# Attention before a mixture of experts: keys loaded two units at a time, their zeros kept in place, and the order of the steps of a unit changed

## The chip, the core and the metric

The kernel runs on one core of a Trainium2 chip. The core has five engines that run on their own and meet at semaphores: TensorE (PE in the profile; its weight loads are PEld), VectorE (DVE), ScalarE (ACT), GpSimd (POOL) and SyncE (SP, which here only issues transfers). Each engine takes its instructions strictly in the order in which they are written. The metric is the time of one execution on the device in microseconds (us); lower is better.

## The reference

Attention over 4 batches of 12 heads, with capped scores, and after it a layer of 8 experts, of which each token uses one:

```python
# q, k, v: (4, 12, 448, 64); cap = 30
scores = q @ k.transpose(0, 1, 3, 2) / sqrt(64)
scores = cap * tanh(scores / cap)
attn = exp(scores - scores.max(-1)) / sum
x = (attn @ v).transpose(0, 2, 1, 3).reshape(1792, 768)

e_idx = argmax(x @ w_gate, 1)          # one expert of 8 per token
h = relu(x[mask] @ w1[e])              # 768 -> 1024
out[mask] = gate_w * eom * (h @ w2[e]) # 1024 -> 768
```

## The kernel before

**Attention** goes over 24 units u; a unit is two heads of one batch (p and p + 6), which lie on the lower and upper 64 partitions. The scores are held with keys on the partitions and queries along a row: 448 keys are three chunks of 128 and a rest of 64. The rests of the two heads are put together into one chunk of 128 whose keys for the other head are zeros, and that is why the key planes have 512 columns and two blocks of zeros. A unit takes these steps:

- `load_k`, `load_q`, `load_v` issue transfers, nearly all from SP. Keys and queries are fetched in pieces of 32 columns (128 bytes), so that DVE can turn them with 32x32 transposes. Queries come for two units in four issues, keys for one unit in six: the rest of the second head is two issues of its own, since it goes to another place in the row than in the tensor. The zeros of the key tiles `kks` are written once, by DVE.
- `t_k(u)` and `t_q(u)` on DVE: one transpose into PSUM (`turned`), one cast to the plane `hi`, one subtraction for `lo` (`planes_of`). The table `TURN` says how many of these run ahead of the unit, before and after the value products. There are five sets of planes.
- `qk(u, s)` on PE: three products (hi·hi, lo·hi, hi·lo) into a PSUM tile, then tanh on ACT (line 369). After the rest, s = 3, one exp over the whole unit follows (line 371).
- `pv(u - 1, c)` on PE: the value products of the unit before (line 379), into the tile u, which ACT or DVE copies out (`u_evac`).
- `presum` on POOL adds the chunks of a unit for the row sums, which PE finishes in `sums`.

`scores` and `half` give out three PSUM tiles in a ring: each taker waits until the last reader of the tile three places before is done. The score tiles, the value products and the steps of the router all take from this ring, in the order in which they are written.

**The router** of a batch (`end_of_batch`) is spread over the units of the next batch: `slots` holds functions that run in places named f, g, h, q and e of a unit. A row step `rws[p]` transposes a unit's output on PE (`row_tr`), scales it on DVE (`row_out`, line 579, tile xr) and puts its store to the tensor xs on a list, which `store_rows` issues from SP at the end of the unit. `gts` transposes the router's products, `logits` and `choose` find each token's expert on DVE, and `rank_mm` and `place` its place in a table, which POOL scatters.

**The seam.** During the last units `early` plans the first five blocks of expert work, `fetch_dma` (fd) reads their rows of the table, `load_raw` (lds) starts the weights from SP, and `gather` on POOL fetches the tokens out of xs. From there on PE multiplies weights that ACT and DVE split into planes (lines 1039, 1040 and 1061).

The main loop and the functions around the change:

Of the kernel before, what the change touches and what calls it, by code (L numbers as in the profile page):

```python
# [22 lines left out]
def tile_kernel(ctx: ExitStack, tc, q, k, v, cap, w_gate, w_ogate, w1, w2, out):  # L23
# [35 lines left out]
    TURN = {6: (1, 2), 8: (1, 2), 10: (2, 2), 13: (1, 2), 14: (1, 2), 15: (1, 2), 16: (1, 2)}  # L59
    KD = DM // 128  # L60
    KF = DFF // 128

# [15 lines left out]
    plp = att.enter_context(tc.tile_pool(name="plp", bufs=5))  # L78
# [20 lines left out]
    BK = 4 * NK  # L99
    NB = S // 32  # L100
# [19 lines left out]
    def load_tails(dst, src, eng):  # L120
        for j in range(2):
            eng.dma_start(out=dst[64 * j:64 * j + 64, NK, j], in_=src[j, SK:S])

    def load_first():
        k_, q_ = heads(k, 0), heads(q, 0)
        load_natural(k0, k_, NK, 128, (nc.sync, nc.scalar))
        load_tails(k0, k_, nc.scalar)
        load_natural(q0, q_, NCH, CP, (nc.sync, nc.scalar))

    def pieces(dst, src, c, eng):  # L130
        x = c % 2
        eng.dma_start(out=dst[32 * c:32 * c + 32],
                      in_=src[:, 32 * x:32 * x + 32].rearrange("(r b) a -> b r a", b=32))

    def load_k(u):
        if u >= NU:
            return
        t, src = kks[u % 4], heads(k, u)
        for c in range(2):
            pieces(t[:, 0:NB], src[0], c, nc.sync)  # L140
        for c in range(2, 4):
            pieces(t[:, 0:BK], src[1, 0:SK], c, nc.sync)
        for c in range(2, 4):
            pieces(t[:, BK + 2:BK + 4], src[1, SK:S], c, nc.sync)

    def load_q(u):
        if u >= NU:
            return
        t = raw1[3 + u // 2 % 3][:, 0:2 * S].rearrange("p (h r a) -> p h r a", h=2, a=32)
        lo = 1 - u % 2  # L150
        for c in range(4):
            h = c // 2 * NP + u % NP
            pieces(t[:, 1 - lo:].rearrange("p h r a -> p (h r) a"), q[u // NP, h:h + lo + 1].rearrange("h s d -> (h s) d"), c, nc.sync)
        for i in range(1 - lo, 2):
            ldq[u + i - (1 - lo)] = t[:, i]

    def load_v(u, eng):
# [9 lines left out]
    zero(k0, nc.vector)  # L167
    load_first()
    for t in kks:
        zero_k(t, nc.vector)  # L170
# [28 lines left out]
    for t in vvs:  # L199
        zero(t, nc.gpsimd)  # L200
# [88 lines left out]
    def part_tile(nm, shape):  # L289
        return plp.tile(shape, F32R, tag=nm, name=nm)  # L290
# [9 lines left out]
    def planes_of(u, ps, nm, n):  # L300
        hi, lo = part_tile(nm + "H", [128, n]), part_tile(nm + "L", [128, n])
        copy(u == 0, hi, ps)
        minus(lo, ps, hi)
        return [hi, lo]

    def t_k(u):
        pl[u] = planes_of(u, turned(kks[u % 4], SK + 128), "K", SK + 128)

    def t_q(u):
        pl[u] += planes_of(u, turned(ldq.pop(u), S), "Q", S)  # L310

    loads = [f for u in range(2, NU) for f in ((load_k, u), (load_q, u)) if f[0] is load_k or u % 2 == 0]
# [27 lines left out]
    def prep_first():  # L340
        pk = tbank([128, SK + 128], "tk0")
        for c in range(NK + 1):
            nc.tensor.transpose(pk[:, c * 128:(c + 1) * 128], k0[:, c].rearrange("p j d -> p (j d)"), ident)
# [3 lines left out]
        pl[0] = planes_of(0, pk, "K", SK + 128) + planes_of(0, pq, "Q", S)  # L347
        scales()


    def qk(u, s):
        KH, KL, QH, QL = pl[u]
        if s == 0:
            pt[u] = ptp.tile([128, 2 * NK + 1, S], F32, tag="pt", name="pt")
        n = 2 if s < NK else 1
        sl = slice(s * 128, (s + 1) * 128)
        if s < NK:
            ps = scores("s")
            for i, (x, y) in enumerate(((KH, QH), (KL, QH), (KH, QL))):
                for j in range(2):  # L360
                    h = slice(64 * j, 64 * j + 64)
                    nc.tensor.matmul(ps[:, j, 0:S], lhsT=x[h, sl], rhs=y[h], start=(i == 0), stop=(i == 2))  # L362
            ps = ps[:, :, 0:S]
        else:
            ps = half("s3")[:, 0:S]
            for i, (x, y) in enumerate(((KH, QH), (KL, QH), (KH, QL))):
                nc.tensor.matmul(ps, lhsT=x[:, sl], rhs=y, start=(i == 0), stop=(i == 2))
            ps = ps.unsqueeze(1)
        nc.scalar.activation(out=pt[u][:, 2 * s:2 * s + n], in_=ps, func=ACTF.Tanh, scale=icap)  # L369
        if s == NK:  # L370
# [69 lines left out]
    def end_of_batch(b):  # L440
# [164 lines left out]
        elif b == B - 2:  # L605
# [732 lines left out]
```

## Time and profile before

| | us |
|---|---|
| three timed runs | 552.52, 554.72, 557.71; median 554.72 |
| the profiled execution | 550.1 |
| its span, first to last instruction | 548.1 |
| PE busy in the span | 502.3 (92%) |
| DVE, ACT, POOL busy | 371.8, 370.3, 284.8 |

The profiled execution is one run; its span is the time between its first and last instruction, and 2.0 us lie around it. In the 40 slices of the profile's page PE is at 9 tenths or more from the middle of the span to shortly before its end, and between 6 and 9 tenths before that; so the page already tells the attention and the experts apart.

### The profile page before, as it was taken

To read this page: it belongs to the slowest core of one execution; us is meant where nothing else is said; L and a number is where in the kernel's file an instruction comes from. 1 tells how busy PE (TensorE), PEld (TensorE's weight loads), DVE (VectorE), ACT (ScalarE), POOL (GpSimd) and SP (SyncE) were. 2 spreads that over 40 slices of the span, in tenths; PEclk is the share of its full clock that TensorE was granted. 3 is DMA by queue.
4 is the path that set the end of the run, shared out by engine and by line. 5 is a ranking of instruction groups with operands and counts; after the bars stand their busy time and mean duration, and the time that the engine had idled before them with its cause. 6 is when DMAs were issued, how large, how long until landed. Compare 5 with 4: busy or idle time off the path is not lost. (4 is left out here: it accounts for less than half of the span.)

```text
span 548.1 us, 10151 instructions
## 1 busy us (share of the span) xinstructions
PE 502.3 (92%) x3077; PEld 346.7 (63%) x3077; DVE 371.8 (68%) x629; ACT 370.3 (68%) x425; POOL 284.8 (52%) x342
## 2 busy tenths in 40 slices
PE   7899799797787979879999999999999999999994
PEld 6354355344333545347899997997879977666692
DVE  5666588685785468348999888786758594546460
ACT  6899578587475667553657987886858686556551
POOL 8999677769665840235715686222637125252001
PEclk9999799899888989979999999999999999999998
DMA  6645565666662224497707932617958959893001
GB/s 137 116 92 101 102 111 109 112 116 94 117 110 61 52 39 80 124 407 200 225 2 287 397 132 88 238 59 256 358 183 308 405 217 387 330 347 133 0 30 47
DMA packets 157772, 91.93 MB, mean 168 GB/s; under 512 B 140418, under 2 KB 140554, under 8 KB 157712
## 3 DMA queue, kind: packets, MB, share of 16 engines
q1 hardware_dynamic: 145792, 57.79, 40.2%
q0 software_dynamic: 8832, 32.74, 16.3%
q10 hardware_dynamic: 3088, 0.71, 0.6%
q8 instruction: 26, 0.43, 0.3%
q14 instruction: 34, 0.28, 0.1%
HBM read 123.68 MB, written 12.04 MB: 248 GB/s over the span
## 5 line engine op out<-in xcount | busy, mean ns | idle before, releaser
L1040 DVE TENSOR_TENSOR wr<-raw,wr 128x768 fp32r<-128x768 f32 (+1 forms) x167 | 171.9, 1066 | 70.0 <-ACT wr L1039 62.4
L1039 ACT ACTIVATE wr<-raw 128x768 fp32r<-128x768 f32 (+1 forms) x167 | 150.4, 935 | 35.9 <-DMA raw<-in_moe_w_dram 12.1
L369 ACT ACTIVATE pt<-s,icap 128x896 f32<-128x896 f32 x96 | 82.2, 912 | 37.3 <-PE s L362 19.9
L379 PE MATMUL u<-pt,vv 128*64 128x448 f32 x384 | 85.5, 591 | 12.3 <-DVE xr L579 6.8
L1061 PE MATMUL py<-wr,hh 128*128 128x384 f32 x352 | 77.3, 340 | 0.0
L1061 PE MATMUL php<-wr,xh 128*128 128x512 f32 x264 | 75.6, 408 | 0.0
L371 ACT ACTIVATE pt<-pt,capc 128x3136 f32<-128x3136 f32 x24 | 69.9, 2911 | 0.8
L1130 POOL DMA_INDIRECT out_dram<-yo,ti x13 | 19.3, 1488 | 95.7 <-ACT yo L1128 72.8
L379 PEld LDWEIGHTS u<-pt,vv 128*64 128x64 f32 x384 | 28.2, 148 | 60.0 <-issue 45.5
L1061 PEld LDWEIGHTS py<-wr,hh 128*128 128x128 f32 x352 | 61.2, 188 | 4.0 <-issue 3.7
L390 POOL TENSOR_TENSOR pa<-pt 128x896 f32<-128x896 f32 x20 | 42.0, 2100 | 27.5 <-ACT pt L371 25.8
L1061 PEld LDWEIGHTS php<-wr,xh 128*128 128x128 f32 x264 | 47.9, 190 | 13.0 <-issue 3.6
L297 DVE STREAM_TRANSPOSE tk<-raw 128x512 f32<-128x512 f32 (+1 forms) x46 | 31.7, 689 | 24.3 <-DMA raw<-in_k_dram 15.5
L391 POOL TENSOR_TENSOR pb<-pa,pt 128x896 f32<-128x896 f32 x20 | 42.0, 2101 | 10.2 <-PE sm L421 8.8
L395 POOL TENSOR_TENSOR pb<-pb,pt 64x448 f32<-64x448 f32 x40 | 45.5, 1137 | 3.1
L1061 PE MATMUL py<-wr,hl 128*128 128x384 f32 x176 | 44.8, 335 | 0.0
L1061 PE MATMUL php<-wr,xl 128*128 128x512 f32 x132 | 41.9, 398 | 0.0
L362 PE MATMUL s<-QH,KH 64*128 64x448 f32 x144 | 30.1, 408 | 7.7 <-DVE ut L402 4.0
L1177 POOL DMA_DIRECT2D rh<-in_moe_w_dram x42 | 23.2, 554 | 22.9 <-DVE wr L1040 13.6
L1061 PEld LDWEIGHTS py<-wr,hl 128*128 128x128 f32 x176 | 31.8, 188 | 0.0
L362 PEld LDWEIGHTS s<-QH,KH 64*128 64x128 f32 x144 | 14.2, 188 | 23.7 <-issue 9.2
L1061 PEld LDWEIGHTS php<-wr,xl 128*128 128x128 f32 x132 | 25.0, 190 | 6.1
(252 smaller groups left out, 788.5 us busy)
## 6 DMA issues: line engine op xcount, KB each, us to landing
raw<-in_moe_w_dram SPq DMA_DIRECT2D x78, 512.0 KB
raw<-in_moe_w_dram SPq DMA_DIRECT2D x104, 384.0 KB
rh<-in_moe_w_dram POOLq DMA_DIRECT2D x18, 512.0 KB
rh<-in_moe_w_dram POOLq DMA_DIRECT2D x24, 384.0 KB
raw<-in_q_dram SPq DMA_DIRECT2D x45, 112.0 KB
vv<-in_v_dram SPq DMA_DIRECT2D x44, 96.0 KB
xs<-xr SPq DMA_DIRECT2D x36, 112.0 KB
raw<-in_k_dram SPq DMA_DIRECT2D x46, 56.0 KB
```

The source lines that it names most:

```text
L297: nc.vector.transpose(out=ps, in_=src.rearrange("p r a -> p (r a)"))
L362: nc.tensor.matmul(ps[:, j, 0:S], lhsT=x[h, sl], rhs=y[h], start=(i == 0), stop=(i == 2))
L369: nc.scalar.activation(out=pt[u][:, 2 * s:2 * s + n], in_=ps, func=ACTF.Tanh, scale=icap)
L371: nc.scalar.activation(out=pt[u], in_=pt[u], func=ACTF.Exp, scale=capc)
L379: nc.tensor.matmul(ups[u][64 * j:64 * j + 64], lhsT=V[:, c, j, :], rhs=P[:, 2 * c + (j if c < NK else 0)], start=(c == 0), stop=(c == NK))
L390: eng.tensor_tensor(out=a, in0=P[:, 0:2], in1=P[:, 2:4], op=ALU.add)
L391: eng.tensor_tensor(out=s1[u], in0=a, in1=P[:, 4:6], op=ALU.add)
L395: eng.tensor_tensor(out=s1[u][h, j], in0=s1[u][h, j], in1=P[h, 2 * NK], op=ALU.add)
L1039: nc.scalar.activation(out=t[:, 0, 0:F], in_=raw, func=ACTF.Copy)
L1040: nc.vector.tensor_tensor(out=t[:, 1, 0:F], in0=raw, in1=t[:, 0, 0:F].bitcast(F32), op=ALU.subtract)
L1061: nc.tensor.matmul(ps[g][:, 0:n], lhsT=st[:, c], rhs=w[:, z, g * n:(g + 1) * n], start=(c == 0 and st is hi and z == 0), stop=(c == (KD, K ...
L1177: nc.gpsimd.dma_start(out=d, in_=rows_of(src, e, w, c), **kw)
```

## The change

1. **Keys.** `load_pair` loads keys as queries were loaded: two units in four issues, into raw1[0] to raw1[2] (they were in raw2[4] to raw2[7]). It may run five units ahead of the turns (keys three, queries four before).
2. **Zeros.** The key planes become ten fixed tiles whose two zero blocks POOL writes once. `k_planes` turns 448 columns instead of 512, and copies and subtracts them in three parts each: 384 columns on all partitions, and twice 64 columns on half of them.
3. **Values.** Two tiles of two units each instead of three of one; the tails of two units come in two issues, so that two units take six issues instead of eight.
4. **Order of a unit.** The rest's products `qk(u, 3)` and their tanh follow directly on the other three; the exp (`expo`) stays behind slots f and g. `TURN` gives its third turn to unit 5 instead of unit 13.
5. **Seam.** `gts`, `logits` and `choose` of the third batch move from places q and e to h of unit 19, ahead of the value products; the row step of p = 5 moves from unit 22 (f) to unit 21 (q), with its store; one step of `early` runs a place sooner.

The diff, cut to its core:

```diff
--- before.py
+++ after.py
-    TURN = {6: (1, 2), 8: (1, 2), 10: (2, 2), 13: (1, 2), 14: (1, 2), 15: (1, 2), 16: (1, 2)}
+    TURN = {5: (1, 2), 6: (1, 2), 8: (1, 2), 10: (2, 2), 14: (1, 2), 15: (1, 2), 16: (1, 2)}
...
-    kks = [raw2[4 + i][:, 0:SK + 128].rearrange("p (r a) -> p r a", a=32) for i in range(4)]
-    vvs = [ldp.tile([128, NK + 1, 2, D], F32, name=f"vv{i}", bufs=1) for i in range(3)]
-    ldq = {}
+    vvs = [ldp.tile([128, 2, NK + 1, 2, D], F32, name=f"vv{i}", bufs=1) for i in range(2)]
+    ldk, ldq = {}, {}
...
-    def pieces(dst, src, c, eng):
-        x = c % 2
-        eng.dma_start(out=dst[32 * c:32 * c + 32],
-                      in_=src[:, 32 * x:32 * x + 32].rearrange("(r b) a -> b r a", b=32))
+    def load_pair(src, u, base, to):
+        t = raw1[base + u // 2 % 3][:, 0:2 * S].rearrange("p (h r a) -> p h r a", h=2, a=32)
+        lo = u % 2
+        for c in range(4):
+            x = c % 2
+            h = c // 2 * NP + u % NP
+            nc.sync.dma_start(
+                out=t[32 * c:32 * c + 32, lo:].rearrange("p h r a -> p (h r) a"),
+                in_=src[u // NP, h:h + 2 - lo, :, 32 * x:32 * x + 32].rearrange("h (r b) a -> b (h r) a", b=32))
+        for i in range(lo, 2):
+            to[u + i - lo] = t[:, i]
 
     def load_k(u):
-        if u >= NU:
-            return
-        t, src = kks[u % 4], heads(k, u)
-        for c in range(2):
-            pieces(t[:, 0:NB], src[0], c, nc.sync)
-        for c in range(2, 4):
-            pieces(t[:, 0:BK], src[1, 0:SK], c, nc.sync)
-        for c in range(2, 4):
-            pieces(t[:, BK + 2:BK + 4], src[1, SK:S], c, nc.sync)
+        load_pair(k, u, 0, ldk)
...
+    def v_tails(u, eng):
+        for j in range(2):
+            h = j * NP + u % NP
+            eng.dma_start(out=vvs[u // 2 % 2][64 * j:64 * j + 64, :, NK, j],
+                          in_=v[u // NP, h:h + 2, SK:S].rearrange("h p d -> p h d"))
+
+    def load_v(u):
         if u < NU:
...
+            v_main(u, nc.sync)
+            v_tails(u, nc.sync)
+            v_main(u + 1, nc.sync)
...
-    for t in kks:
-        zero_k(t, nc.vector)
...
+    kpl = [[plp.tile([128, SK + 128], F32R, name=f"K{i}{z}", bufs=1) for z in "HL"] for i in range(PB)]
+    for hl in kpl:
+        for t in hl:
+            nc.gpsimd.memset(t.bitcast(F32)[0:64, SK + 64:], 0.0)
+            nc.gpsimd.memset(t.bitcast(F32)[64:128, SK:SK + 64], 0.0)
...
+    def k_planes(u, ps):
+        hi, lo = kpl[u % PB]
+        parts = [(hi[:, 0:SK], lo[:, 0:SK], ps[:, 0:SK])]
+        for j in range(2):
+            h, c = slice(64 * j, 64 * j + 64), slice(SK + 64 * j, SK + 64 * j + 64)
+            parts.append((hi[h, c], lo[h, c], ps[h, SK:S]))
+        for x, _, y in parts:
+            copy(u == 0, x, y)
+        for x, z, y in parts:
+            minus(z, y, x)
+        return [hi, lo]
...
-            if u > (tdone[t_k] + 3 if f is load_k else tdone[t_q] + 4):
+            if u > tdone[t_k if f is load_k else t_q] + 5:
...
-        if s == NK:
-            nc.scalar.activation(out=pt[u], in_=pt[u], func=ACTF.Exp, scale=capc)
+
+    def expo(u):
+        nc.scalar.activation(out=pt[u], in_=pt[u], func=ACTF.Exp, scale=capc)
...
-            at = {(-1, "q"): [g0], (0, "f"): [P(sums, EARLY), g1, sums_out], (0, "h"): [t[1]], (0, "q"): gts,
-                  (0, "e"): [logits, choose],
+            at = {(-1, "q"): [g0], (0, "f"): [P(sums, EARLY), g1, sums_out], (0, "h"): [t[1], *gts, logits, choose],
                   (1, "g"): [rank_mm, place, rws[0]], (1, "h"): [place2, enter, scatter], (1, "q"): [rws[1]],
-                  (1, "e"): [nx] * 2,
-                  (2, "g"): [rws[2], rws[3]], (2, "h"): [nx] * 2, (2, "q"): [rws[4]], (2, "e"): [*[nx] * 2, P(set_known, NE)],
-                  (3, "f"): [fd[0], fd[1], *lds[:2], rws[5], store_rows],
+                  (1, "e"): [nx] * 3,
+                  (2, "g"): [rws[2], rws[3]], (2, "h"): [nx], (2, "q"): [rws[4], rws[5]], (2, "e"): [*[nx] * 2, P(set_known, NE)],
+                  (3, "f"): [fd[0], fd[1], *lds[:2]],
...
     for u in range(NU):
-        if u > 2:
-            load_v(u + 1, nc.sync)
+        if u > 2 and u % 2:
+            load_v(u + 1)
         for s in range(NK):
             qk(u, s)
         load_ahead()
+        qk(u, NK)
         before, after = TURN.get(u, (1, 1))
         turn_next(before)
         if 0 < u <= NU - 4:
             presum(u - 1, 1)
         slot(u, "f")
         slot(u, "g")
-        qk(u, NK)
+        expo(u)
```

On PE, at unit 11 (two row steps in place g, trow), before; s is a score tile, s_1289 the rest's, u the value products, sm the row sums:

```order
L362 MATMUL s<-QH,KH 128x448 x2
L362 MATMUL s<-QH,KL 128x448 x2
L362 MATMUL s<-QL,KH 128x448 x2
L574 MATMUL trow<-ident,ut 112x128 x8
L367 MATMUL s_1289<-QH,KH 128x448
L367 MATMUL s_1289<-QH,KL 128x448
L367 MATMUL s_1289<-QL,KH 128x448
L379 MATMUL u<-pt,vv_121 64x448 x8
L421 MATMUL sm<-pb,ohc 32x448 x4
```

The same place of the changed kernel:

```order
L364 MATMUL s<-QH,K1H 128x448 x2
L364 MATMUL s<-QH,K1L 128x448 x2
L364 MATMUL s<-QL,K1H 128x448 x2
L369 MATMUL s_1257<-QH,K1H 128x448
L369 MATMUL s_1257<-QH,K1L 128x448
L369 MATMUL s_1257<-QL,K1H 128x448
L577 MATMUL trow<-ident,ut 112x128 x8
L382 MATMUL u<-pt,vv_121 64x448 x8
L424 MATMUL sm<-pb,ohc 32x448 x4
```

The two row steps now stand between the rest's products and the value products, no longer ahead of the rest.

On DVE, one turn of keys (tk is the transposed tile) and what follows it in unit 10, before:

```order
L297 STREAM_TRANSPOSE tk<-raw_4_116 128x512
L287 CAST KH<-tk 128x512
L293 TENSOR_TENSOR KL<-tk,KH 128x512
L297 STREAM_TRANSPOSE tk<-raw_3_109 128x448
L287 CAST QH<-tk 128x448
L293 TENSOR_TENSOR QL<-tk,QH 128x448
```

And a turn of keys in the changed kernel, in the same unit:

```order
L286 STREAM_TRANSPOSE tk<-raw_0_106 128x448
L276 CAST K3H<-tk 128x384
L276 CAST K3H<-tk 64x64 x2
L282 TENSOR_TENSOR K3L<-tk,K3H 128x384
L282 TENSOR_TENSOR K3L<-tk,K3H 64x64 x2
L500 TENSOR_TENSOR gm<-pg,rec 112x192 x4
```

Three instructions have become seven.

On SP, from unit 21 on to the first weights, before (tc is a block's rows of the table, raw a chunk of weights); the reads of meta between them are left out:

```order
L586 DMA xs<-xr 112x4x64 x6
L118 DMA vv_122<-in_v_dram 128x3x64 x2
L122 DMA vv_122<-in_v_dram 64x64 x2
...
L836 DMA tc<-tab_105 128x2
...
L813 DMA raw_0_106<-in_moe_w_dram 128x1024
...
L813 DMA raw_1_107<-in_moe_w_dram 128x1024
L586 DMA xs<-xr 112x4x64 x2
```

And in the changed kernel:

```order
L108 DMA vv_121<-in_v_dram 128x3x64 x2
L589 DMA xs<-xr 112x4x64 x8
...
L838 DMA tc<-tab_105 128x2
...
L815 DMA raw_0_106<-in_moe_w_dram 128x1024
...
L815 DMA raw_1_107<-in_moe_w_dram 128x1024
```

The last two stores of xs now stand before the table's rows and the first weights, and no value load stands between.


## Rows read from the trace of the kernel before

**Rows 1.** The stretches view: busy us of each engine, granted clock, DMA share.

```profile
core 0: us, PE busy (x) PEld busy (x) DVE busy (x) ACT busy (x) POOL busy (x), PEclk, DMA share, GB/s
...
82.00:126.00 44.00, 39.54 (x246) 19.45 (x242) 34.87 (x70) 32.98 (x31) 31.75 (x23) 0.96 0.60 109
126.00:156.00 30.00, 23.37 (x135) 11.83 (x135) 19.79 (x34) 19.62 (x18) 20.43 (x13) 0.94 0.65 107
156.00:200.00 44.00, 34.94 (x194) 17.51 (x192) 26.36 (x68) 26.48 (x28) 29.47 (x21) 0.88 0.33 64
...
262.00:500.00 238.00, 238.00 (x1525) 197.97 (x1525) 181.50 (x250) 173.32 (x231) 109.87 (x150) 1.00 0.67 247
```

**Rows 2.** The timeline of ACT: start us, us, then [idle before <-releaser].

```profile
28.06 3.31 ACT L369 ACTIVATE pt<-s,icap 128x896 f32<-128x896 f32 x4
...
45.25 2.91 ACT L371 ACTIVATE pt<-pt,capc 128x3136 f32<-128x3136 f32 x1
...
52.24 2.91 ACT L371 ACTIVATE pt<-pt,capc 128x3136 f32<-128x3136 f32 x1
...
63.98 2.91 ACT L371 ACTIVATE pt<-pt,capc 128x3136 f32<-128x3136 f32 x1
...
222.27 2.91 ACT L371 ACTIVATE pt<-pt,capc 128x3136 f32<-128x3136 f32 x1
```

**Rows 3.** The timeline of PE at the value products of five units.

```profile
81.14 3.23 PE L379 MATMUL u<-pt,vv 128*64 128x448 f32 x16
...
99.98 4.67 PE L379 MATMUL u<-pt,vv 128*64 128x448 f32 x16 [2.29 <-DVE xr L579]
...
140.91 4.68 PE L379 MATMUL u<-pt,vv 128*64 128x448 f32 x16 [4.53 <-DVE xr L579]
...
161.06 4.84 PE L379 MATMUL u<-pt,vv 128*64 128x448 f32 x16 [2.15 <-issue]
...
173.74 4.92 PE L379 MATMUL u<-pt,vv 128*64 128x448 f32 x16 [2.31 <-issue]
```

**Rows 4.** The timeline of DVE, three of its steps on keys and queries.

```profile
81.83 0.62 DVE L287 CAST QH<-tk 128x448 fp32r<-128x448 f32 x1
...
138.02 0.73 DVE L297 STREAM_TRANSPOSE tk<-raw 128x512 f32<-128x512 f32 x1 [2.65 <-DMA raw<-in_k_dram]
...
171.47 0.69 DVE L287 CAST KH<-tk 128x512 fp32r<-128x512 f32 x1 [6.19 <-PE s L367]
```

**Rows 5.** The waits of the whole run: total us, times, longest us.

```profile
DVE tk L297 <- DMA raw<-in_k_dram: 15.5, 9, 3.1
...
ACT pt L369 <- PE s L367: 10.3, 11, 1.6
```

**Rows 6.** The timeline of POOL: the last zeroing of value tails, and sums.

```profile
2.21 0.14 POOL L113 MEMSET vv<- 64x64 f32 x1
2.39 0.15 POOL L114 MEMSET vv<- 64x64 f32 x1
...
25.40 2.36 POOL L395 TENSOR_TENSOR pb<-pb,pt 64x448 f32<-64x448 f32 x2
```

**Rows 7.** The source view of line 132, SP's issues: ns min/median/max.

```profile
L132 SPq DMA_DIRECT2D raw<-in_k_dram x138: 311/469/1711, 1.9 to 160.1; - x138
```

**Rows 8.** The timeline of all engines at the seam to the experts.

```profile
194.86 0.22 PE L527 MATMUL trk<-ohb,tri 112*112 112x32 bf16 x1 [3.20 <-DVE ohb L517]
...
223.48 0.91 SPq L586 DMA_DIRECT2D xs<-xr  x2
...
229.80 2.00 POOL L851 DMA_INDIRECT xg<-xs,ti  x1 [8.89 <-DMA tc<-tab]
...
234.20 1.06 ACT L1039 ACTIVATE wr<-raw 128x1024 fp32r<-128x1024 f32 x1 [5.13 <-DMA raw<-in_moe_w_dram]
...
236.99 1.54 PE L863 MATMUL pt_x<-ident,xg 128*128 128x128 f32 x6 [5.39 <-DMA xg<-xs,ti]
...
238.14 0.87 ACT L864 ACTIVATE xh<-pt_x 128x512 fp32r<-128x512 f32 x2 [2.45 <-PE pt_x L863]
```

More of the change, by code (lines that the diff above doesn't have):

```diff
@@ L58, in tile_kernel @@
     UACT = 8
-    TURN = {6: (1, 2), 8: (1, 2), 10: (2, 2), 13: (1, 2), 14: (1, 2), 15: (1, 2), 16: (1, 2)}
+    TURN = {5: (1, 2), 6: (1, 2), 8: (1, 2), 10: (2, 2), 14: (1, 2), 15: (1, 2), 16: (1, 2)}
     KD = DM // 128
     KF = DFF // 128
+    PB = 5
     ctx.enter_context(tc.manual_schedule())
@@ L77, in tile_kernel @@
     att = ExitStack()
-    plp = att.enter_context(tc.tile_pool(name="plp", bufs=5))
+    plp = att.enter_context(tc.tile_pool(name="plp", bufs=PB))
     ldp = att.enter_context(tc.tile_pool(name="ldp", bufs=2))
@@ L118, in load_natural @@
             engs[j].dma_start(out=dst[:, 0:n, j], in_=src[j, 0:n * m].rearrange("(c p) d -> p c d", c=n))
-    def load_tails(dst, src, eng):
-        for j in range(2):
-            eng.dma_start(out=dst[64 * j:64 * j + 64, NK, j], in_=src[j, SK:S])
     def load_first():
@@ L126, in load_first @@
         load_natural(k0, k_, NK, 128, (nc.sync, nc.scalar))
-        load_tails(k0, k_, nc.scalar)
+        nc.scalar.dma_start(out=k0[0:64, NK], in_=k_[:, SK:S].rearrange("j p d -> p j d"))
         load_natural(q0, q_, NCH, CP, (nc.sync, nc.scalar))
-    def pieces(dst, src, c, eng):
-        x = c % 2
-        eng.dma_start(out=dst[32 * c:32 * c + 32],
-                      in_=src[:, 32 * x:32 * x + 32].rearrange("(r b) a -> b r a", b=32))
-    def load_k(u):
-        if u >= NU:
-            return
-        t, src = kks[u % 4], heads(k, u)
-        for c in range(2):
-            pieces(t[:, 0:NB], src[0], c, nc.sync)
-        for c in range(2, 4):
-            pieces(t[:, 0:BK], src[1, 0:SK], c, nc.sync)
-        for c in range(2, 4):
-            pieces(t[:, BK + 2:BK + 4], src[1, SK:S], c, nc.sync)
@@ L146, in load_q @@
-    def load_q(u):
[L147 to L157, printed above, removed]
+    def load_pair(src, u, base, to):
[9 more added lines that the diff above has]
+            to[u + i - lo] = t[:, i]
@@ L158, in load_v, with v_main @@
+    def load_k(u):
+        load_pair(k, u, 0, ldk)
+    def load_q(u):
+        load_pair(q, u, 3, ldq)
+    def v_main(u, eng):
+        load_natural(vvs[u // 2 % 2][:, u % 2], heads(v, u), NK, 128, (eng, eng))
+    def v_tails(u, eng):
[4 more added lines that the diff above has]
+    def load_v(u):
         if u < NU:
-            v_ = heads(v, u)
@@ L199, in tile_kernel @@
     for t in vvs:
-        zero(t, nc.gpsimd)
+        nc.gpsimd.memset(t[0:64, :, NK, 1], 0.0)
+        nc.gpsimd.memset(t[64:128, :, NK, 0], 0.0)
+    kpl = [[plp.tile([128, SK + 128], F32R, name=f"K{i}{z}", bufs=1) for z in "HL"] for i in range(PB)]
[3 more added lines that the diff above has]
+            nc.gpsimd.memset(t.bitcast(F32)[64:128, SK:SK + 64], 0.0)
     load_k(1)
@@ L298, in turned, with q_planes @@
         return ps
-    def planes_of(u, ps, nm, n):
-        hi, lo = part_tile(nm + "H", [128, n]), part_tile(nm + "L", [128, n])
+    def q_planes(u, ps):
+        hi, lo = part_tile("QH", [128, S]), part_tile("QL", [128, S])
         copy(u == 0, hi, ps)
@@ L304, in planes_of @@
         return [hi, lo]
+    def k_planes(u, ps):
[9 more added lines that the diff above has]
+        return [hi, lo]
     def t_k(u):
-        pl[u] = planes_of(u, turned(kks[u % 4], SK + 128), "K", SK + 128)
+        pl[u] = k_planes(u, turned(ldk.pop(u), S))
     def t_q(u):
-        pl[u] += planes_of(u, turned(ldq.pop(u), S), "Q", S)
-    loads = [f for u in range(2, NU) for f in ((load_k, u), (load_q, u)) if f[0] is load_k or u % 2 == 0]
+        pl[u] += q_planes(u, turned(ldq.pop(u), S))
+    loads = [f for u in range(2, NU, 2) for f in ((load_k, u), (load_q, u))]
     tdone = {t_k: 0, t_q: 0}
@@ L340, in prep_first @@
     def prep_first():
-        pk = tbank([128, SK + 128], "tk0")
+        pk = tbank([128, S], "tk0")
         for c in range(NK + 1):
-            nc.tensor.transpose(pk[:, c * 128:(c + 1) * 128], k0[:, c].rearrange("p j d -> p (j d)"), ident)
+            n = min(128, S - c * 128)
+            nc.tensor.transpose(pk[:, c * 128:c * 128 + n], k0[0:n, c].rearrange("p j d -> p (j d)"), ident[0:n, 0:n])
         pq = scores("tq0")[:, 0, 0:S]
@@ L346, in prep_first @@
             nc.tensor.transpose(pq[:, c * CP:(c + 1) * CP], q0[:, c].rearrange("p j d -> p (j d)"), ident[0:CP, 0:CP])
-        pl[0] = planes_of(0, pk, "K", SK + 128) + planes_of(0, pq, "Q", S)
+        pl[0] = k_planes(0, pk) + q_planes(0, pq)
         scales()
@@ L366, in qk @@
             for i, (x, y) in enumerate(((KH, QH), (KL, QH), (KH, QL))):
-                nc.tensor.matmul(ps, lhsT=x[:, sl], rhs=y, start=(i == 0), stop=(i == 2))
+                nc.tensor.matmul(ps, lhsT=x[:, SK:], rhs=y, start=(i == 0), stop=(i == 2))
             ps = ps.unsqueeze(1)
         nc.scalar.activation(out=pt[u][:, 2 * s:2 * s + n], in_=ps, func=ACTF.Tanh, scale=icap)
-        if s == NK:
-            nc.scalar.activation(out=pt[u], in_=pt[u], func=ACTF.Exp, scale=capc)
+    def expo(u):
+        nc.scalar.activation(out=pt[u], in_=pt[u], func=ACTF.Exp, scale=capc)
     def pv(u, c):
         P = pt[u]
-        V = vvs[u % 3]
+        V = vvs[u // 2 % 2][:, u % 2]
         if c == 0:
@@ L967, in tile_kernel @@
         slot(u, "g")
-        qk(u, NK)
+        expo(u)
         if u < 2:
-            load_v(u, nc.scalar)
-        if 0 < u < 3:
-            load_v(u + 1, nc.sync)
+            v_main(u, nc.scalar)
+        if u == 0:
+            v_tails(u, nc.scalar)
+        if u == 1:
+            load_v(2)
         if u > NU - 4:
```

11 lines of the change are left out of this document (removed).

## The prediction, made before the changed kernel ran

> **What bounds the kernel now.** I read the stretches of the span first, then ACT's timeline for the pace of the units, then PE's for its gaps, and last what DVE, POOL and SP were doing at each gap. From 262 to 500 us PE is busy in all 238 us at full clock [rows 1], so the experts cost what they cost, and whatever the attention saves moves the whole of it forward. Up to 228 us no engine is full: between 82 and 200 us PE is busy 39.5 of 44, 23.4 of 30 and 34.9 of 44 us, DVE 34.9, 19.8 and 26.4, ACT and POOL no more than 33 [rows 1]. Units wait there for each other's steps. The last exp starts at 222.27 us [rows 2].
>
> PE's gaps have a pattern. [...] Before, the ring goes s0, s1, s2, row, row, rest, u, so u gets the tile of the first row step and waits until DVE has scaled it; DVE in turn stood behind a turn of keys, which had waited 2.65 us for its transfer (138.02), or for the rest's products to free a key plane (6.19 us, at 171.47) [rows 4].
>
> **The change part by part.**
>
> *Rest ahead of the slots.* Now the ring goes s0, s1, s2, rest, row, row, u: u gets the rest's tile, free as soon as its tanh is done, and xr is wanted only by the next unit's first score tile, one set of value products (3.23 us) later. The plane that DVE waited 6.19 us for is also freed earlier, since the row step no longer stands ahead of the rest. The four gaps cost 2.29 + 1.44, 4.53 + 1.45, 2.15 + 1.61 and 2.31 + 1.69, together 17.5 us (the second number of each is the length above 3.23). PE's whole idle time in the three stretches is 4.5 + 6.6 + 9.1 = 20.2 us, so these are most of it. I take two thirds, 11.7, because the next unit's s0 still waits for xr where DVE is late; the ends are 8 and 17.5. ACT's own wait for the rest, 10.3 us in 11 waits [rows 5], I count at nothing beside it: PE was transposing rows in that time and has to do so in any order. If ACT and not PE were the limit, it would be a gain of up to 10.3.
>
> *Keys in pairs.* Per two units SP issues 4 instead of 12 transfers of keys and 6 instead of 8 of values. At 0.469 us each [rows 7] that is 4.7 us of SP's time per two units. The descriptors stay pieces of 128 bytes and the bytes stay the same, so the transfers themselves get no shorter; what ends DVE's waits for keys (15.5 us in 9 waits [rows 5]) is that a pair may be fetched five units ahead instead of three. DVE's waits are paid in the gaps above and not again: 0. [...]
>
> *Three-part planes.* A cast of 448 columns takes 0.62 us and one of 512 takes 0.69 [rows 4]: 0.0011 us a column and 0.13 fixed. By that 384 columns are 0.55 and 64 are 0.20 (estimates; no row has such a piece of a plane). A turn of keys goes from 0.73 + 2 × 0.69 = 2.11 to 0.66 + 2 × (0.55 + 0.40) = 2.56 us, the 0.66 being 0.73 less 64 columns. Over 23 units DVE does 10.4 us more. DVE was busy 81.0 of 118 us between 82 and 200 [rows 1], so some two thirds of the time; work added to an engine with that much idle time mostly lies beside PE's. I charge 4; the ends are 0 and 10.4.
>
> *Zeros on POOL.* 24 zeroings instead of 6, one every 0.18 us [rows 6]: POOL's sums start 18 × 0.18 = 3.2 us later. POOL sets the pace of units 3 to 6: its sum ended at 25.40 + 2.36 = 27.76 us and the tanh of unit 3 that waits for the buffer began at 28.06 [rows 2, 6]. So these units run 3.2 us later. Before, unit 7 took 63.98 − 52.24 = 11.74 us from exp to exp [rows 2], where unit 6, at POOL's pace, took 52.24 − 45.25 = 6.99. Earlier turns (unit 5) and earlier keys should take that excess of 4.8 away; net of the 3.2 this gives −1.6. The ends are −1.6 and +3.2, if unit 7 still stalls by as much.
>
> *Seam, choice of experts.* At unit 20 PE waited 3.20 us for the choice [rows 8]. It now starts a place earlier, beside the value products. In exchange PE meets the sums' transposes at once after ACT has copied the sums out, behind the rest's tanh; I estimate 1.0 for that from the 0.62 us of a 448-column instruction and its way. Net −2.2, between −3.2 and +1.
>
> *Seam, last row.* The first gather waited 8.89 us and began at 229.80 us, because the last stores of xs were issued at 223.48, behind the first weights [rows 8]. PE then waited 5.39 us for its tokens, and ACT split them at 238.14. Now these stores go out a unit sooner, without a value load between. The gather is then ready before PE is, and the next thing that is late is the third chunk of weights: ACT, in order, splits it at 234.20 until 235.26 [rows 8], and that chunk comes up to 0.9 us earlier with two stores fewer ahead of it. From 238.14 to about 234.6 is 3.5 us. Ends 0 and 5.4.
>
> *The rest* (one issue instead of two for the first key tails; DVE's ten zeroings gone; expert weights into other buffers): DVE and those buffers were idle then, so nothing.
>
> **Sum.** −11.7 − 1.6 − 2.2 − 3.5 + 4.0 = −15.0 us. The profiled execution took 550.1 us, so 535.1 in its terms. The three timed runs lie higher (median 554.72), and I set the difference against that: 554.72 − 15.0 = 539.7.
>
> **Rivals.** *The wait moves one tile on.* DVE is late by more than 3.23 us in the units with row steps, PE stops at the next s0 instead of at u, and keys arrive as late as before because the DMA engines are no less busy. For it: DVE has more to do, and it waits in order. Against: the four waits at u were 2.2 to 4.5 us long, so at most one would outlive the shift whole. Price: a third of 17.5 (−6), nothing at unit 7 and in the choice, −1.5 at the gather, +4 for DVE: −3.5, 551.2 us.
>
> *Nearly every gap goes.* 17.5 + 1.6 + 3.2 + 5.4 with DVE's extra work hidden: −27.7, 527.0 us. For it: PE's idle time between 82 and 200 us is as large as the terms. Against: three more engines must all keep up.
>
> *Slower: the small pieces.* No row has a 64-column piece of a plane; if one costs as much as the 448-column instruction (0.62), a turn of keys is 0.66 + 2 × (0.55 + 1.24) = 4.24 us, 2.13 more than before, 49 us over 23 units. With half of that on the path it is 24.5 against gains of 19.0: +5.5, 560.2 us. It decides from a piece of 0.50 us on (23 × (4 × 0.50 + 0.55 × 2 + 0.66 − 2.11) / 2 = 19). Against: the slope of the two casts.
>
> **How the numbers follow.** Forecast 0.55 (532 to 547), nearly every gap 0.18, the wait moves on 0.16, slower 0.11. A measurement of this kernel tells some 1% from no change, here 5.5 us. The first two cases are faster by more than that, and so is 0.02 of the third: 0.75. The rest of the third, 0.14, is within 1%; the last, 0.11, is slower. The range takes in the second case's time and the third's and leaves out the fourth: 526 to 554.
>
> **What would show it.** In the changed profile: value products at 3.2 to 3.3 us in all units, no wait of theirs on xr longer than 0.5 us, and a granted clock near 1 between 82 and 200 us; no wait of DVE for keys after the first three units; 64-column pieces near 0.20 us; tanh of unit 3 near 31.3 us; the last exp near 212 to 214 us; the first gather right after its table rows, and ACT's first split of tokens 12 to 13 us after the last exp (15.9 before). I am wrong if PE's gaps reappear at the first score tile of the units after row steps, if DVE is busy over nine tenths, or if POOL's sums still pace units after the eighth.

## The result, and the profile after

The changed kernel took 541.09 us (median of four runs, 537.80 to 541.76), the kernel before 555.61 us beside it (552.52 to 557.71). The ratio is 0.973, with a 95% interval of 0.967 to 0.979. The forecast was 539.7 us, with a range of 526 to 554. The total came out as worked out, but the runs below show that its largest term did not. The two traces are nearer to each other than the medians: the profiled execution of before, 550.1 us, lies below its timed runs, and that of the changed kernel, 541.76 us, is the slowest of its four, so that 8.3 us lie between them.

The waits that the prediction started from are gone. In the page's groups of the changed kernel (busy, mean ns, then idle time before the group) the value products have 1.3 us of idle time before them in the whole run:

```profile
L382 PE MATMUL u<-pt,vv 128*64 128x448 f32 x384 | 80.5, 563 | 1.3 <-ACT pt L371 0.8
```

On PE's timeline all sets but two take 3.51 us or less, against the four slow ones of [rows 3]; the two are those in unit 2 (4.44 us) and in unit 21 (4.79). But the stretches (columns as in [rows 1]) do not read as they should if PE now ran through:

```profile
82.00:126.00 44.00, 36.68 (x222) 17.99 (x218) 38.30 (x87) 29.91 (x29) 32.50 (x23) 0.92 0.62 111
126.00:156.00 30.00, 29.17 (x183) 15.74 (x183) 27.34 (x62) 25.96 (x23) 23.86 (x15) 1.00 0.34 67
156.00:200.00 44.00, 33.77 (x206) 17.36 (x202) 33.01 (x85) 25.67 (x29) 27.15 (x20) 0.92 0.24 47
...
262.00:500.00 238.00, 237.23 (x1521) 195.85 (x1520) 175.54 (x227) 170.59 (x228) 107.09 (x143) 1.00 0.66 239
```

The middle stretch is full now, 29.17 of 30 us at a granted clock of 1.00, where it was 23.37 [rows 1]. In the first and third PE is busy less than before and its granted clock is 0.92. PE's timeline has the largest gap of each, one long wait:

```profile
117.17 0.74 PE L364 MATMUL s<-QH,K3H 64*128 64x448 f32 x2 [6.29 <-DVE gsb L276]
...
174.87 0.74 PE L364 MATMUL s<-QH,K4H 64*128 64x448 f32 x2 [5.30 <-DVE gsb L276]
```

These are the third score tiles of units 13 and 19. Each takes the ring tile that the router's gate products left (tg, written in place q of the unit before), and that tile is free only when DVE has copied it out (gsb). Two such products, which take 0.47 us at 132.93 us, in the stretch whose granted clock is 1.00, take 0.74 behind these waits. DVE's timeline of the changed kernel tells why the copy is late:

```profile
108.48 0.19 DVE L549 TENSOR_REDUCE pos<-rk 112x4 f32<-112x32 f32 x1
108.70 1.83 DVE L550 CAST posi<-pos 112x4 uint32<-112x4 f32 x1
110.44 0.17 DVE L555 TENSOR_REDUCE den<-ex 112x4 f32<-112x32 f32 x1
110.65 2.03 DVE L556 TENSOR_SCALAR den<-den 112x4 f32<-112x4 f32 x1
...
112.91 0.98 DVE L560 COPY ent<-ids 112x4 f32<-112x4 f32 x1
...
113.87 0.65 DVE L286 STREAM_TRANSPOSE tk<-raw 128x448 f32<-128x448 f32 x1
114.56 0.94 DVE L276 CAST K1H<-tk 128x384 fp32r<-128x384 f32 x3
115.53 0.94 DVE L282 TENSOR_TENSOR K1L<-tk,K1H 128x384 fp32r<-128x384 f32 x3
116.50 0.62 DVE L276 COPY gsb<-tg 128x448 f32<-128x448 f32 x1
```

And POOL's timeline beside it:

```profile
108.39 2.11 POOL L393 TENSOR_TENSOR pa<-pt 128x896 f32<-128x896 f32 x1 [1.74 <-ACT pt L374]
110.58 2.08 POOL L394 TENSOR_TENSOR pb<-pa,pt 128x896 f32<-128x896 f32 x1
112.74 2.32 POOL L398 TENSOR_TENSOR pb<-pb,pt 64x448 f32<-64x448 f32 x2
```

DVE never stands idle here. Three instructions on four numbers a partition take 1.83, 2.03 and 0.98 us, and each ends within 0.1 us of the end of one of POOL's sums (108.39 + 2.11 = 110.50; 110.58 + 2.08 = 112.66; for the third the first half of the last row, 112.74 + 1.16 = 113.90). Then a turn of keys stands ahead of the copy. In the trace of before, the same cast took 0.17 us:

```profile
110.56 0.17 DVE L547 CAST posi<-pos 112x4 uint32<-112x4 f32 x1
```

Ahead of the wait at unit 19, DVE's timeline of the changed kernel has the same kind of steps, and behind them a turn of queries ahead of the copy:

```profile
167.56 1.95 DVE L547 TENSOR_TENSOR rk<-rk,ohb 112x32 f32<-112x32 f32 x1
...
169.76 0.93 DVE L550 CAST posi<-pos 112x4 uint32<-112x4 f32 x1
...
170.81 1.08 DVE L556 TENSOR_SCALAR den<-den 112x4 f32<-112x4 f32 x1
```

### The profile page after: what moved, and what is told of

The parts are those of the page before. It is cut to its first block, busy times and chain, and to the rows that moved or that the text cites. A ratio compares the mean times of both kernels' runs of the same rounds, so it can differ in the third digit from the quotient of the medians.

```text
span 540.2 us, 10059 instructions
## 1 busy us (share of the span) xinstructions
PE 498.9 (92%) x3077; PEld 345.0 (64%) x3077; DVE 391.0 (72%) x713; ACT 369.0 (68%) x427; POOL 289.4 (54%) x360
## 2 busy tenths in 40 slices
DMA packets 155932, 91.93 MB, mean 170 GB/s; under 512 B 138578, under 2 KB 138714, under 8 KB 155872
## 3 DMA queue, kind: packets, MB, share of 16 engines
q1 hardware_dynamic: 144000, 57.78, 40.6%
## 5 line engine op out<-in xcount | busy, mean ns | idle before, releaser
L371 ACT ACTIVATE pt<-s,icap 128x896 f32<-128x896 f32 x96 | 80.8, 914 | 40.8 <-PE s L364 28.0
L382 PE MATMUL u<-pt,vv 128*64 128x448 f32 x384 | 80.5, 563 | 1.3 <-ACT pt L371 0.8
L1135 POOL DMA_INDIRECT out_dram<-yo,ti x13 | 20.5, 1575 | 94.8 <-ACT yo L1133 70.6
L382 PEld LDWEIGHTS u<-pt,vv 128*64 128x64 f32 x384 | 26.3, 142 | 43.5 <-issue 36.5
L398 POOL TENSOR_TENSOR pb<-pb,pt 64x448 f32<-64x448 f32 x40 | 45.6, 1141 | 3.1
L286 DVE STREAM_TRANSPOSE tk<-raw 128x448 f32<-128x448 f32 x46 | 30.1, 655 | 4.9 <-issue 4.0
L1236 POOL DMA_INDIRECT out_dram<-yh,toh x6 | 6.2, 1039 | 32.0 <-issue 8.7
L853 POOL DMA_INDIRECT xg<-xs,ti x14 | 17.2, 1229 | 10.6 <-PE pt_x L865 4.7
```

Of the source, the lines that this page charges most:

```text
L286: nc.vector.transpose(out=ps, in_=src.rearrange("p r a -> p (r a)"))
L398: eng.tensor_tensor(out=s1[u][h, j], in0=s1[u][h, j], in1=P[h, 2 * NK], op=ALU.add)
L1135: nc.gpsimd.indirect_dma_start(out=out, out_offset=bass.IndirectOffsetOnAxis(ap=ti, axis=0), in_=y, in_offset=None, bounds_check=NT - 1, o ...
```

## The experiments

Each kernel is the changed kernel with the edit shown, unless it says otherwise. Times are medians; ratios are to the kernel before, run on the same chip. Beside the different kernels its own median was 554.34 to 555.75 us, so a difference of about one us between two kernels that did not run side by side tells nothing. The table gives, from ACT's timeline of each profiled run, the start of the exp of some units and of the first split of tokens (us):

| kernel | 3 | 7 | 12 | 13 | 18 | 19 | 23 | split | median |
|---|---|---|---|---|---|---|---|---|---|
| before | 31.40 | 63.98 | 110.87 | 118.66 | 172.13 | 185.09 | 222.27 | 238.14 | 555.61 |
| changed | 35.55 | 64.14 | 105.33 | 120.78 | 162.14 | 180.01 | 217.27 | 229.08 | 541.09 |
| rest_early_alone | 33.05 | 65.13 | 107.53 | 123.84 | 169.61 | 186.78 | 222.21 | 239.57 | 548.79 |
| rest_late | 34.69 | 63.27 | 106.76 | 114.56 | 163.15 | 172.37 | 210.58 | 221.33 | 532.48 |
| rest_late_kept | 34.67 | 63.24 | 106.73 | 114.52 | 156.90 | 176.41 | 210.28 | 222.26 | 533.56 |
| keys_before | 31.98 | 65.73 | 107.60 | 121.06 | 162.23 | 178.46 | 215.01 | 225.83 | 537.43 |
| rest_late_keys | 32.09 | 66.30 | 110.39 | 118.18 | 161.82 | 179.29 | 214.20 | 225.75 | 538.21 |
| seam_before | 34.66 | 63.23 | 104.42 | 121.07 | 163.36 | 181.21 | 216.63 | 229.51 | 542.03 |
| rest_late_seam | 34.70 | 63.28 | 106.78 | 114.56 | 156.94 | 176.21 | 214.94 | 227.72 | 538.26 |
| zeros_dve | 32.12 | 62.50 | 103.67 | 120.34 | 161.85 | 179.43 | 214.64 | 225.66 | 536.14 |
| turns_last | 36.28 | 70.56 | 114.02 | 128.02 | 171.97 | 187.94 | 224.07 | 236.13 | 545.72 |

### The kernel before, once more

> The kernel before, unchanged, for a second trace. The profiled execution of before took 550.1 us, 5 less than the median. If the difference lies in the attention, this trace's last exp starts at 224 us or later for a run of 554 us or more; if in the experts, it starts at 222 us as before.

It took 553.44 us; its last exp began at 226.62 and its tokens were split at 242.39, 15.8 us later as in the first trace (15.9). So runs of this kernel differ by some 4 us inside the attention. The trace that the prediction was read from is 4.6 us below the median, and a difference of one or two us between two traces tells nothing.

### The order of the rest

First the order alone, put into the kernel before:

```diff
         load_ahead()
+        qk(u, NK)
...
         slot(u, "g")
-        qk(u, NK)
+        expo(u)
```

> The kernel before with one part of the change alone: the rest's products and tanh ahead of slots f and g. Theory of the ring's order: it alone gives most of the attention's gain, 544 to 549 us against 555.6. Rival (keys): 553 to 557, with DVE's waits for keys still near 15 us in the waits view and PE stopping at the next unit's first score tile instead.

548.79 us, ratio 0.990 (0.987 to 0.993): a gain of 5.5 us, at the small end of what was expected. The waits of the value products are gone here too. PE's longest waits between 82 and 200 us, from the view of waits (total us, times, longest us), are these:

```profile
PE s L362 <- DVE gsb L287: 12.2, 2, 6.8
PE s L362 <- DVE xr L580: 3.6, 2, 3.1
```

Then the reverse, the changed kernel with the order of before:

```diff
-        qk(u, NK)
         before, after = TURN.get(u, (1, 1))
...
         slot(u, "g")
+        qk(u, NK)
         expo(u)
```

> The changed kernel with the rest's products and tanh put back behind slots f and g; all else as changed. Theory (the ring's order gave the gain): the value products of the units with row steps wait for xr again; I expect three or more waits of over 1.5 us on it between 82 and 200 us, and a time of 549 to 554 us, 8 to 13 over the changed kernel's 541. Rival (the earlier keys gave it, the order did not matter): DVE is not late any more, the waits on xr stay under 0.5 us and the time is within 3 us of 541.

532.48 us, ratio 0.961 (0.958 to 0.965): 8.6 us below the changed kernel, where 8 to 13 above was expected. The theory that the order carries the gain falls. This kernel computes the rests of units 17 and 18 with wrong keys: with fixed planes, the keys of units 22 and 23 are turned into their planes ahead of the late rest that still has to read them. A wait is missing there, so its time alone proves nothing. The next kernel keeps the rest of these two units early and computes everything:

```diff
+        if u in (17, 18):
+            qk(u, NK)
...
-        qk(u, NK)
+        if u not in (17, 18):
+            qk(u, NK)
         expo(u)
```

> The changed kernel with the rest back behind slots f and g in all units but 17 and 18, where it stays early, so that no key plane is written before its last reader and the output is the reference's. Theory A (rest early costs time in this kernel, because it moves the row steps and the small steps of the router into the time of POOL's sums, and PE then waits 5 to 6 us for the router's copy gsb at units 13 and 19): 531 to 535 us, ratio 0.957 to 0.965, and exp of unit 13 follows that of unit 12 by 8 to 10 us instead of 15.5. Theory B (the 532 us of the kernel with the rest late came from the overwritten planes, that is from a wait that was missing): 538 to 544 us.

533.56 us (531.87 to 534.18), ratio 0.959 (0.954 to 0.964), against 0.973 (0.967 to 0.979) with the rest early everywhere. Theory B falls, and of theory A it holds that the early rest costs time here through the wait for gsb; this one kernel shows both orders. At unit 13, behind late rests, there is no wait for gsb and exp follows exp by 7.79 us (8 to 10 expected, 15.45 in the changed kernel). At unit 19, behind the early rests of units 17 and 18, it stands as before, 19.51 us from exp to exp:

```profile
169.63 0.74 PE L364 MATMUL s<-QH,K4H 64*128 64x448 f32 x2 [5.46 <-DVE gsb L276]
```

In the kernel with all rests late (rest_late) this wait is missing at unit 19 as well, and exp follows exp there by 9.22 us. The wait at unit 19 stands in the changed kernel and in rest_late_kept alike, so the 7.5 us between them come from unit 13: the changed kernel is 1.40 us ahead at unit 12, 6.26 behind at unit 13 and 6.99 behind at unit 23. DVE's timeline ahead of unit 13 of rest_late_kept:

```profile
105.55 0.97 DVE L547 TENSOR_TENSOR rk<-rk,ohb 112x32 f32<-112x32 f32 x1
...
106.55 0.19 DVE L549 TENSOR_REDUCE pos<-rk 112x4 f32<-112x32 f32 x1
106.77 0.17 DVE L550 CAST posi<-pos 112x4 uint32<-112x4 f32 x1
106.85 0.18 DVE L555 TENSOR_REDUCE den<-ex 112x4 f32<-112x32 f32 x1
107.06 0.17 DVE L556 TENSOR_SCALAR den<-den 112x4 f32<-112x4 f32 x1
...
107.46 0.12 DVE L560 COPY ent<-ids 112x4 f32<-112x4 f32 x1
...
110.39 0.62 DVE L276 COPY gsb<-tg 128x448 f32<-128x448 f32 x1
```

And POOL's, the end of one unit's sums and the start of the next:

```profile
104.12 2.35 POOL L398 TENSOR_TENSOR pb<-pb,pt 64x448 f32<-64x448 f32 x2
109.78 2.13 POOL L393 TENSOR_TENSOR pa<-pt 128x896 f32<-128x896 f32 x1 [3.31 <-ACT pt L374]
```

The first of the small steps (L547) still begins beside a sum and ends with it (106.52 and 106.47); the others now fall between two of POOL's sums and take 0.12 to 0.20 us. L547 starts at 105.55, ahead of the exp at 106.73; in the changed kernel it starts at 108.27, behind the exp at 105.33. With the rest ahead of the slots, the exp and so POOL's sums come sooner, while the router's products on PE, and DVE's steps on them, come later.

### Keys, planes and zeros

The loads, the 512-column planes and the zeros of before in the changed kernel (the planes stay in the fixed tiles here and in rest_late_keys, whose expectation speaks of rotating buffers):

```diff
-        pl[u] = k_planes(u, turned(ldk.pop(u), S))
+        hi, lo = kpl[u % PB]
+        ps = turned(kks[u % 4], SK + 128)
+        copy(False, hi, ps)
+        minus(lo, ps, hi)
+        pl[u] = [hi, lo]
...
-            if u > tdone[t_k if f is load_k else t_q] + 5:
+            if u > (tdone[t_k] + 3 if f is load_k else tdone[t_q] + 5):
```

> The changed kernel with the old keys: one unit in six issues, up to three units ahead, zeros in the loaded tile, planes cast and subtracted 512 wide by one instruction each; order, values and seam as changed. Theory of the ring's order: DVE has some 10 us less to do and waits for keys some 10 to 15 us again; the two nearly cancel, 538 to 545 us, and the gate's copy gsb comes sooner where keys are not late. Rival (keys gave the gain): 548 to 554 us.

537.43 us (536.79 to 538.49), ratio 0.971 (0.967 to 0.974). The medians say that the key part costs 3.7 us; the intervals overlap, so no gain is all that is shown. The same edit with the rest late:

> As rest_late_kept, with the keys of before: loaded unit by unit with zeros in the loaded tile, planes of 512 columns in rotating buffers, POOL zeroing only the first pair of planes. If the key part of the change is a loss whatever the order (some 0.5 us of DVE a turn and 3 us of POOL): 3 to 5 us below rest_late_kept, 527 to 531 us. If keys fetched five units ahead are worth something once the rest is late (a wait of DVE for keys comes back, 15 us in all in the kernel before): 3 to 8 us above it, 535 to 542 us.

538.21 us (536.00 to 540.96), ratio 0.970 (0.964 to 0.976), 4.7 us above rest_late_kept, whose runs all lie below it. There the key part is a gain. What it removes is in the waits of rest_late_keys:

```profile
DVE tk L308 <- DMA raw<-in_k_dram: 15.2, 8, 3.6
```

One of them stands on its DVE timeline at unit 7:

```profile
56.61 0.73 DVE L308 STREAM_TRANSPOSE tk<-raw 128x512 f32<-128x512 f32 x1 [2.23 <-DMA raw<-in_k_dram]
```

Unit 7 takes 11.28 us there from exp to exp, and 7.96 in rest_late_kept; all of the 3.66 us by which unit 12 is later has come by unit 8 (4.63 there). With the rest early unit 7 takes 11.47 us in keys_before, against 8.39 in the changed kernel. With the rest early the lead of the new keys is lost again: keys_before is 2.27 us behind the changed kernel at unit 12 and 0.28 at unit 13, since the wait for gsb takes it up (4.52 instead of 6.29 us).

The zeros of the key planes written by DVE instead of POOL:

```diff
-            nc.gpsimd.memset(t.bitcast(F32)[0:64, SK + 64:], 0.0)
+            nc.vector.memset(t.bitcast(F32)[0:64, SK + 64:], 0.0)
```

> The changed kernel with the zeros of the key planes written by DVE instead of POOL. POOL's sums then start 3 us sooner, tanh of units 2 and 3 at 21.5 and 28.5 us instead of 24.58 and 32.19. If POOL's start was a real cost that is never given back: 537 to 539 us. If unit 13's wait absorbs it: 540 to 542 us. If DVE's 20 zeroings (about 3.5 us) hold up unit 0's planes: 541 to 544.

536.14 us (534.84 to 538.11), ratio 0.967 (0.963 to 0.971): 5.0 us below the changed kernel by the medians, while the intervals of the ratios overlap. Exp of unit 3 starts 3.4 us sooner, but only 1.7 of it reaches unit 12, and 0.4 unit 13. With the rest late:

> As rest_late_kept, with the zeros of the key planes written by DVE instead of POOL. If the two gains are in different stretches (units 2 to 8 and units 12 to 20) they add: 5 us below rest_late_kept, 526 to 531 us. If POOL's sums only set the pace of the first units until something else does, or if the steps fall into other phases: within 1.5 us of rest_late_kept.

532.73 us (531.57 to 537.34), ratio 0.958 (0.954 to 0.963): no difference to rest_late_kept. What is gained with the rest early is thus not a price of the zeroing as such.

### Turns behind the copy

If DVE's turn of keys stands between the small steps and gsb, one can move it behind:

```diff
-        turn_next(after)
...
             u_evac(u - 1)
+        turn_next(after)
```

> The changed kernel with the turns that stand behind the value products moved behind the router's copies and u_evac, so that DVE copies the gate's tile gsb (and u) before it turns keys and queries. Theory (what is left of the attention's idle time is the wait of a score tile for gsb, 6.29 and 5.30 us in the changed profile, a turn of 2.5 us of it): these waits fall by 2.5 us or more each, the units 1 to 8 get u sooner, 533 to 538 us. Rival: DVE is full and only the order of its lateness changes, 539 to 544 us.

> Both of the two others. If they add: 530 to 536 us. If both remove time that the same later wait absorbs: as the better of the two.

545.72 us (ratio 0.982, 0.975 to 0.988) and, with the zeros on DVE, 542.45 us (0.978, 0.975 to 0.981): slower by 4.6 us than the changed kernel (all runs lie above its runs, though the intervals of the ratios overlap) and by 6.3 us than zeros_dve. The waits for gsb shrink to 6.0 us in 2, but now the turns stand behind a copy that waits for PE, and PE waits for queries. PE's timeline of turns_last has such a wait in each of the units 2 to 6, two of which are:

```profile
31.78 0.47 PE L364 MATMUL s<-QH,K3H 64*128 64x448 f32 x2 [2.07 <-DVE QH L276]
...
48.84 0.74 PE L364 MATMUL s<-QH,K0H 64*128 64x448 f32 x2 [2.20 <-DVE QH L276]
```

And DVE's timeline there has the copies that wait for the value products:

```profile
38.18 0.62 DVE L405 COPY ut<-u 128x448 f32<-128x448 f32 x1 [3.25 <-PE u L382]
...
46.72 0.62 DVE L405 COPY ut<-u 128x448 f32<-128x448 f32 x1 [3.26 <-PE u L382]
```

Exp of unit 7 starts at 70.56 us, 6.4 us later than in the changed kernel.

### The seam

The seam steps of before in the changed kernel:

```diff
-            at = {..., (0, "h"): [t[1], *gts, logits, choose],
+            at = {..., (0, "h"): [t[1]], (0, "q"): gts, (0, "e"): [logits, choose],
...
-                  (2, "q"): [rws[4], rws[5]], ...
-                  (3, "f"): [fd[0], fd[1], *lds[:2]],
+                  (2, "q"): [rws[4]], ...
+                  (3, "f"): [fd[0], fd[1], *lds[:2], rws[5], store_rows],
```

> The changed kernel with the third batch's router steps and the last row step in their old places. By my sum it loses 2.2 + 3.5 us: 545 to 548 us; the first gather then begins again 13 us or more after the last exp started instead of about 8, PE waits 3 us or more for its first tokens, and at unit 20 PE waits about 3 us for the choice. Rival: the weights' loads set the start of the experts either way, 540 to 542 us.

542.03 us, ratio 0.979 (0.975 to 0.982): 0.9 us by the medians and 3 by the ratios, whose intervals overlap, so not to be told from none. Its waits for the choice and for the first tokens are 1.47 and 2.47 us, not the 3 that were expected of each. With the rest late:

> As rest_late_kept, with the seam steps of before (choice of experts in q and e of unit 19, last row step in unit 22, one planning step later). If the seam steps carry their price of 4 to 6 us once the attention ends earlier: 536 to 540 us. If they are worth as little as with the rest early (about 1 us): 532 to 535 us.

538.26 us (536.86 to 538.73), ratio 0.968 (0.963 to 0.973): 4.7 us above rest_late_kept. PE's timeline of rest_late_seam has both waits of [rows 8], the second shorter:

```profile
185.98 0.22 PE L530 MATMUL trk<-ohb,tri 112*112 112x32 bf16 x1 [3.19 <-DVE ohb L520]
...
227.02 0.93 PE L866 MATMUL pt_x<-ident,xg 128*128 128x128 f32 x6 [2.75 <-DMA xg<-xs,ti]
```

In rest_late_kept the first is 0.87 us, and in place of the second PE waits for ACT, which on its timeline stands behind the weights:

```profile
220.88 1.06 ACT L1047 ACTIVATE wr<-raw 128x1024 fp32r<-128x1024 f32 x1 [3.41 <-DMA raw<-in_moe_w_dram]
221.84 0.53 ACT L403 ACTIVATE ut<-u 128x448 f32<-128x448 f32 x1
222.26 0.59 ACT L866 ACTIVATE xh<-pt_x 128x512 fp32r<-128x512 f32 x1
```

## Why the prediction was right, and where it was not

**The rest ahead of the slots, −11.7: wrong in size alone, wrong in sign beside the other parts.** Alone it is worth −5.5 us; in the changed kernel it costs 7.5 (541.09 against 533.56). The cost goes with the parts beside it: early against late, the ratios are 0.973 and 0.959 in the changed kernel, 0.979 and 0.968 with the old seam, 0.967 and 0.958 with the zeros on DVE, but 0.971 and 0.970, no difference, with the old keys. That the value products would no longer wait held. What failed is the reason for taking two thirds: the next taker of a late tile was said to be s0, waiting for xr. It was the third score tile, behind the gate's copy, in two of the units: 11.6 us of waits in place of the 12.3 that the page of before has ahead of the value products, and behind each wait products that take 0.74 us instead of 0.47. The lengths above 3.23 us that the sum adds to the four waits are in [rows 3], but that a wait is what lengthens the products behind it was the author's estimate, and what sets the granted clock no run shows: forecast near 1 between 82 and 200 us, its mean was 0.92, 1.00 and 0.92, lower in the two stretches that hold the waits of 6.29 and 5.30 us. The last exp, forecast near 212 to 214 us, began at 217.27. The rival "the wait moves one tile on" came nearest to this; what excluded more of it, that waits of 2.2 to 4.5 us hardly outlive 3.23 us, assumed that DVE's steps keep their lengths. The sign "PE's gaps reappear at the first score tile of units after row steps" was nearly the right one to watch.

**Keys in pairs, 0: under-sized.** With the rest late the key part as a whole is worth 4.7 us. The text had put DVE's waits for keys, 15.5 us, into PE's gaps; 15.2 us of them come back in rest_late_keys, and what they cost is in units 6 to 8, which take 2.3, 3.3 and 1.6 us longer than in rest_late_kept, and not in those gaps. Of the two causes given for unit 7, turns and keys, it is the key part: rest_late_keys has the new `TURN` and still takes 11.28 us. In the changed kernel the list of DVE's waits names no transfer of keys. The DMA share fell from 0.65 to 0.34 between 126 and 156 us [rows 1] and rose from 0.58 to 0.84 between 14 and 52 us, which fits fetches that run further ahead; the queue has 144000 packets instead of 145792 for the same 57.8 MB, so the pieces are as small as before (138578 of the page's packets are under 512 bytes, 140418 before), and no run shows a shorter transfer.

**Three-part planes, +4: the instruction was sized rightly.** The 64-column casts take 0.205 to 0.228 us (0.20 estimated), the 384-column ones 0.558; three in a row take 0.94, so a turn is 0.66 + 2 × 0.97 = 2.6 us (2.56 estimated). The rival of the small pieces falls. DVE is busy 391.0 us instead of 371.8, more than the 10.4 of the planes, POOL's part in it included. What of it lies on the path was not isolated from the loads.

**Zeros on POOL, −1.6.** The late start is there: tanh of unit 3 began at 32.19 us (31.3 said). Unit 7 still takes 8.39 us, so 3.35 of its 4.8 us of excess went, and its exp started at 64.14 instead of 63.98: about 0 where −1.6 was taken, inside the bounds. What the zeroing costs by itself depends on the order: zeros_dve is 5.0 us below the changed kernel by the medians, rest_late_zeros_dve no different from rest_late_kept.

**Seam, −2.2 and −3.5.** From the last exp to the first split 11.8 us went by (12 to 13 said, 15.9 before), and at its end ACT stands behind a chunk of weights, as was said (3.81 us of wait at 227.69). But with the old places it is 12.9 us in seam_before and 12.8 in rest_late_seam, so the moved steps account for about 1 of these 4 us, and the rest came with the other parts. Ahead of the products that need the choice PE waits 0.87 us, for a tanh, instead of 3.20. As a part of the time this is 4.7 us with the rest late, near the 5.7, but not split as said: between the traces of rest_late_seam and rest_late_kept 1.9 us come at unit 20 (2.2 said for the choice), 2.9 in units 21 to 23 and 0.8 behind the last exp (3.5 said for the last row). Beside the rest early it is only 0.9. The waits of seam_before are shorter there, and the changed kernel loses its lead over it between units 20 and 23 (190.42 to 217.27 us, 26.85; 192.20 to 216.63, 24.43). PE's timeline of the changed kernel has most of that loss at unit 21, a gap of 1.23 us at 199.02, one of 0.54 us and value products that take 4.79 us, where those of seam_before take 3.23:

```profile
200.21 4.79 PE L382 MATMUL u<-pt,vv 128*64 128x448 f32 x16 [0.54 <-ACT pt L371]
```

What held PE up there, and whether it does so in every run, stays open.

**The sum.** −15.0 was said and −14.5 came. That the total was right is luck, for the errors cancelled: 22.2 us are to be had (rest_late_kept), and the order gave 7.5 of them back. Of the 22.2, keys and seam are 4.7 each by their own runs. Some 12.8 are left to the values in pairs, the new `TURN`, the early rests of units 17 and 18 and what the parts do together; no run took these apart, and this stays open. That the wait for gsb carries the price of the early rest is shown by unit 13 of rest_late_kept; that POOL's sums stretch DVE's steps ahead of that copy is read from the ends of their rows, and a kernel without these sums was not run.

The best kernel is rest_late_kept, 533.56 us, 0.959 (0.954 to 0.964); with DVE's zeros it is the same.

## What to carry to other kernels

When a ring of tiles is re-ordered, list for every taker which reader frees its tile, in the units where rare steps (here the router's) take part; the wait went here not to the next in line but to the third score tile, whose reader was late (6.29 and 5.30 us for gsb). Test each part both alone and beside the others: here the seam is worth 0.9 or 4.7 us, and the order gains 5.5 or costs 7.5, depending on the parts beside it. Work that is moved behind a copy also inherits what the copy waits for: in turns_last DVE's turns came behind waits of 3.25 us for PE, and PE then waited 2.2 us for queries.

## What was unexpected in the hardware

In the changed kernel, small DVE instructions with all operands in SBUF that began 0.05 to 0.65 us into one of POOL's sums, or into one half of its last (L398), took 0.93 to 2.03 us, and each ended within 0.1 us of the end of that sum or half; between two sums such instructions took 0.12 to 0.17 us in rest_late_kept (106.77 to 107.74 us). It held for a cast (1.83 us), a copy (0.98) and a scalar operation with one tensor as input (2.03), and for a product (1.95) and a comparison (1.91) of two. Where both began within 0.02 us the trace has either outcome: the product og took 0.19 us at 102.06, with POOL's sum from 102.05, and cand (L645) 1.19 us at 187.36, with POOL's from 187.35. Reductions to four numbers a partition ran beside POOL at 0.17 to 0.19 us, and so did a reciprocal at 0.20, a scalar operation on one number a partition (epsc, L181) at 0.15, and casts and subtractions that read PSUM, at 0.62 and 0.94 us. What makes the one kind wait for POOL and not the other no run here shows.
